# A new opening for a state-space scan with a feed-forward block: load order, halved first weights, top words on GpSimd

## The chip, the cores and the metric

The kernel runs on one core of a Trainium2 chip. The metric is the device time of one execution in microseconds (us). A core has five engines that each work through a queue of their own in order: PE (TensorE, the matrix array, with its weight loads shown as PEld), DVE (VectorE), ACT (ScalarE), POOL (GpSimd) and SP (SyncE, which here only issues DMAs). SBUF is the working memory of 128 partitions; PSUM is the memory of eight banks into which PE writes.

## The reference

A chunked scan (`mamba2_ssd`) is followed by a feed-forward block with a hard swish. Batch is 4, heads 8, sequence 768, head dimension 32, state 16; the feed-forward block has 3072 tokens, 256 model and 2048 hidden features.

```
for c in range(nc):                                  # chunks of 32 tokens
    cum = np.cumsum(la, axis=-1)                     # la = log(clip(a, 1e-6, 1))
    L = np.exp(cum[:, :, :, None] - cum[:, :, None, :]) * causal
    CB = np.einsum('bhin,bhjn->bhij', Cc, Bc)
    y_intra = np.einsum('bhij,bhjd->bhid', CB * L, xc)
    y_inter = np.einsum('bhin,bhnd->bhid', Cc, state) * np.exp(cum)[:, :, :, None]
    y[:, :, sl] = y_intra + y_inter
    state = decay_full * state + sum_j(B_j x_j * decay_from_j)
h = y_as_tokens @ w_in
out = (h * np.clip(h + 3, 0, 6) / 6) @ w_out
```

The weights `w_in` and `w_out` arrive as 64-bit floating-point numbers. The kernel sees them as pairs of 32-bit words and makes 32-bit floats of them itself.

## The kernel before

The sequence is cut into six chunks of 128 tokens, each worked in two halves of 64. For chunk c, DVE and ACT form the decays `L` (differences of cumulated logarithms, then an exponential), PE multiplies the turned B and C into the scores `cb`, DVE multiplies `L` by `cb` (L563), and PE multiplies the result with x (`mix`) and adds what comes from the state (`from_state`). ACT copies the sums y into `yT` (`keep`, L602). The feed-forward block of chunk k follows: for k = 0 it is `mlp_in` (L610, 16 hidden slices f, each with the ramp of the hard swish on ACT, L688, and its product on DVE, L693) and then `first_out` (L707). For later chunks it is done in a form with fewer products (L652 and L766), into which the scan of the next chunk is woven. The order on every engine is written out by hand: what is emitted first is first in its engine's queue.

The opening is what comes before the first `mlp_in`. Its parts are these.

- *Loads.* SP issues a, then C of chunk 0 in eight copies (`pairs_first`, L100, one for each batch and parity of the head), then x (L118) and weight pieces (L139). ACT's queue issues weight piece 0 and B ahead of its table load.
- *Differences.* `diff_mask` (L336) writes the causal mask into a PSUM bank with a matmul, `diff_less` (L348) and `diff_pick` (L357) add the differences of the logarithms, which `in_three` has split into three bf16 parts, and `diff_exp` (L365) takes the exponential. Chunk 0 uses the banks f0 to f3, chunk 1 the banks of the tags o, y0 and y1. `mask_again` (L343) writes masks a second time while PE has nothing else to do.
- *Decoding weights.* `decode(i)` makes piece i of eight (0 to 3 of `w_in`, four slices f each, 4 to 7 of `w_out`). A piece has 1024 numbers on each partition. `weights(i, n)` takes n further steps of it. ACT copies the top 16-bit word of each number (L198), DVE masks exponent and sign (L215, L217), makes the upper significand (L201) and adds the lower one (L205), ACT makes the scale in two activations (L221, L223), DVE puts the sign in (L228) and multiplies (L236). Three raw pieces fit in memory, so the load of piece i+3 waits for piece i.
- *Turning.* PE transposes B (L422), ACT copies it to `bT` (L431). DVE transposes C in squares of 32 (L465) and separates the heads of a pair into `cT` (L472). `first_eto` makes the decays from the start of the chunk, and `fade` multiplies them onto C on GpSimd (L478).

The order of the first steps in the code before is

```
weights(0, 1)
scores(0)
multiply(0)
load_w(3)
c_ps = ps.tile([P, NC, G], FP32, name="c_ps", tag="f1")
turn_cum(c_ps)
busy(1, ps.tile([P, NB * P], FP32, name="d", tag="f0"))
weights(0, 1)
weights(1, 1)
by_token(c_ps)
mix(0)
keep(0)
```

where `busy` is a matmul of the identity by itself (L490) and `turn_cum` (L316) turns the cumulated logarithms of the later chunks.

Of the kernel before, what the change touches and what calls it, by code (L numbers as in the profile page):

```python
# [20 lines left out]
def kernel(  # L21
# [63 lines left out]
    def load_bc(c):  # L85

        sl = slice(c * P, (c + 1) * P)

        def tokens_first(src, queue=nc.sync, **where):
            t = loads.tile([P, NB * NH, N], FP32, **where)
            queue.dma_start(out=t, in_=src[:, :, sl, :].rearrange("b h s n -> s (b h) n"))
            return t

        def pairs_first(src):
            t = loads.tile([P, 2, NB, 4, N], FP32, name="pairs", tag="bc")
            for b in range(NB):
                for h in range(2):
                    nc.sync.dma_start(  # L100
                        out=t[:, h, b].rearrange("s a n -> s (a n)"),
                        in_=src[b, h:NH:2, sl, :].rearrange("h (s a) n -> h s (a n)", a=4))
            return t

        if 0 < c < TURN:
            bcs[c] = [tokens_first(C, name="C", tag="bc")]
        Bs[c] = tokens_first(B, nc.scalar if c == 0 else nc.sync, name="B")
        if c == 0:
            bcs[c] = [pairs_first(C), Bs[c]]
        elif c < TURN:  # L110
            bcs[c].append(Bs[c])
        else:
            bcs[c] = [pairs_first(C), pairs_first(B)]
# [11 lines left out]
    NRAW = 3  # L125
    raws = {}

    def load_w(i, queue=nc.sync):

        raw = loads.tile([P, NK * FP * 2 * P], U32, name="raw", bufs=NRAW)  # L130
        if i < NP:
            cols = slice(2 * i * FP * P, 2 * (i + 1) * FP * P)
            src = moe_w_in[:, cols].rearrange("(k p) f -> p k f", p=P)
            dst = raw.rearrange("p (k f) -> p k f", k=NK)
        else:
            r0 = (i - NP) * FP * P
            src = moe_w_out[r0:r0 + FP * P, :].rearrange("(k p) m -> p k m", p=P)
            dst = raw.rearrange("p (k m) -> p k m", k=FP)
        queue.dma_start(out=dst, in_=src)  # L139
        raws[i] = raw  # L140

    load_w(0, nc.scalar)
    load_bc(0)
    load_x(0)
    load_w(1)
    nc.scalar.preload_act_table_set("natural_log_exp_and_others")


    ident = const.tile([P, P], FP32, name="ident")
# [37 lines left out]
    def decode(i):  # L187

        n = NK * FP * P
        top = raws[i].bitcast(U16).rearrange("p (n w) -> p n w", w=4)[:, :, 3]
        lo, hi = (raws[i].rearrange("p (n w) -> p n w", w=2)[:, :, w] for w in range(2))
        s = att.tile([P, n], U16, name="ws")
        e = att.tile([P, n], U16, name="we")
        m = att.tile([P, n], U32, name="wm")
        nc.scalar.copy(out=s, in_=top)  # L198

        def significand():  # L200
            nc.vector.tensor_scalar(  # L201
                out=m, in0=hi, scalar1=0xFFFFF, scalar2=0x100000,
                op0=ALU.bitwise_and, op1=ALU.bitwise_or)
            yield
            nc.vector.scalar_tensor_tensor(  # L205
                out=m.bitcast(FP32), in0=lo, scalar=2.0 ** -32, in1=m, op0=ALU.mult,
                op1=ALU.add)
            yield

        parts_m = significand()  # L210
        if i == 0:
            next(parts_m)
            next(parts_m)
        yield
        nc.vector.tensor_scalar(  # L215
            out=e, in0=s, scalar1=0x7FF0, scalar2=None, op0=ALU.bitwise_and)
        nc.vector.tensor_scalar(  # L217
            out=s, in0=s, scalar1=0x8000, scalar2=None, op0=ALU.bitwise_and)
        next(parts_m, None)
        yield  # L220
        nc.scalar.activation(e.bitcast(BF16), e, AF.Relu, bias=bias_hi, scale=-8.0)  # L221
        yield
        nc.scalar.activation(e, e.bitcast(BF16), AF.Relu, bias=bias_lo, scale=-1.0)  # L223
        next(parts_m, None)
        if i and i + NRAW < 2 * NP:
            load_w(i + NRAW)
        yield
        nc.vector.tensor_tensor(out=e, in0=e, in1=s, op=ALU.bitwise_or)  # L228
        m, e = m.bitcast(FP32), e.bitcast(BF16)
        if i < NP:  # L230
            dst = w_in[:, :, i * FP * P:(i + 1) * FP * P]
            m, e = (t.rearrange("p (k f) -> p k f", k=NK) for t in (m, e))
        else:
            dst = w_out[:, (i - NP) * FP:(i - NP + 1) * FP, :]
            m, e = (t.rearrange("p (k f) -> p k f", k=FP) for t in (m, e))
        nc.vector.scalar_tensor_tensor(  # L236
            out=dst, in0=m, scalar=2.0 ** -20, in1=e, op0=ALU.mult, op1=ALU.mult)

    pick = const.tile([P, G], BF16, name="pick")
    less = const.tile([P, G], BF16, name="less")
# [29 lines left out]
    def in_three():  # L273
        first = cum[:, :2 * P]
        part = split.rearrange("g c p -> g (c p)")
        nc.vector.tensor_copy(part[:G], first)
        nc.vector.tensor_tensor(out=low, in0=first, in1=part[:G], op=ALU.subtract)
        nc.vector.tensor_copy(mid, low)
        nc.vector.tensor_copy(part[G:2 * G], mid)
        nc.vector.tensor_tensor(out=part[2 * G:pad], in0=low, in1=mid, op=ALU.subtract)  # L280

    cum_d = dram.tile([NC, 2, G, HT], FP32, name="cum_d")
# [44 lines left out]

    def diff_mask(c, b):

        if c == 0:  # L330
            d = ps.tile([P, NH, HT], FP32, name="d", tag=f"f{b}")
        elif b < 2:
            d = ps_o.tile([P, NH, HT], FP32, name="d", tag="o")
        else:
            d = ps_y.tile([P, NH, HT], FP32, name="d", tag=f"y{b % 2}")
        nc.tensor.matmul(  # L336
            out=d, lhsT=ident_h, rhs=hide.unsqueeze(1).to_broadcast([P, NH, HT]),
            start=True, stop=True)
        ds[c, b] = d

    def mask_again(c, b):

        nc.tensor.matmul(  # L343
            out=ds[c, b], lhsT=ident_h, rhs=hide.unsqueeze(1).to_broadcast([P, NH, HT]),
            start=True, stop=True)

    def diff_less(c, b):
        nc.tensor.matmul(  # L348
# [153 lines left out]
                    rhs=csT[pair, b, HALF[a]], start=(a == 0 and b == 0), stop=True,  # L502
                    tile_position=(32 * q, d0), skip_group_check=True)

    def scores(c):

# [1 line left out]

        bT, cT, _ = bTs[c]
        cbs[c] = [ps.tile([P, NB, 2, HT], FP32, name="cb", tag=f"f{q}") for q in range(NQ)]
        both = [ps_y.tile([P, 2, NB, HT], FP32, name=f"y{u}", tag=f"y{u}") for u in range(2)]
        ys[c] = {(0, u): both[u][:, 0] for u in range(2)}
        sps[c] = [both[a if c else 1 - a][:, 1] for a in range(2)]
        if c:
            from_state(c, 0)
        for b in range(NB):
            for a, rows in enumerate(HALF):
                for q in range(NQ):  # L520
# [2 lines left out]
                        out=cbs[c][q][rows, b], lhsT=bT[pair, b, rows],  # L523
                        rhs=cT[pair, b, :, rows], start=(b == 0), stop=True,
                        tile_position=(32 * q, a * HT), skip_group_check=True)
        into_state(c, 0, 1)

    def into_state(c, *halves):
        xt, bs = xts[c], bss[c]
# [44 lines left out]
            op=ALU.mult)  # L574
        new_state(states[c], adds[c], later)

    def mix(c):


        xt = xts[c]  # L580
# [2 lines left out]
        for u in range(2):  # L583
# [7 lines left out]
                            tile_position=(a * HT, d0), skip_group_check=True)  # L591
            if c == 0:
                from_state(c, 1, (2 * u, 2 * u + 1))
        if c:
            from_state(c, 1)

    def keep(c):

        yTs[c] = att.tile([P, NK, NB, P], FP32, name="yT")
        for a, u in ((0, 0), (0, 1), (1, 0), (1, 1)) if c else ((0, 0), (1, 0), (0, 1), (1, 1)):  # L600
            y, dst = ys[c][a, u], yTs[c][:, u, :, HALF[a]]
            nc.scalar.copy(out=dst, in_=y)  # L602

# [243 lines left out]
            for b in bs:  # L847
                part(c, b)

    for c in range(2):  # L850
        for b in range(NB):
            diff_mask(c, b)
    for sl in ends_at:
        log_a(sl)
    row_signs()
    add_up(ends_at[0])
    in_three()
    for b in range(2):
        mask_again(0, b)
    diff(0, 0, 1)  # L860
    diff(0, 2, 3)
    weights(0, 1)
    for b in range(NB):
        diff_exp(0, b)
    first_eto()
    diff(1, 2, 3)
    weights(0, 1)
    for b in range(NB):
        ends(0, b)
    turn_b(0)  # L870
    diff(1, 0, 1)
    weights(0, 1)
    diff_exp(1, 2)
    diff_exp(1, 3)
    turn_squares(bcs[0][0], turned(0)[2])
    part_heads(0)
    fade(0, HALF[1], nc.gpsimd)
    add_up(ends_at[1])
    store_rows()
    load_w(2)  # L880
    weights(0, 1)
    scores(0)
    multiply(0)
    load_w(3)
    c_ps = ps.tile([P, NC, G], FP32, name="c_ps", tag="f1")
    turn_cum(c_ps)
    busy(1, ps.tile([P, NB * P], FP32, name="d", tag="f0"))
    weights(0, 1)
    weights(1, 1)
    by_token(c_ps)  # L890
    mix(0)
    keep(0)
    weights(1, 3)
    renew(0)
    weights(1, 1)
    load_eto(1)
    load(1)


    weave = {}  # L900
# [4 lines left out]
    for k in range(NC):  # L905
        gTs[k] = ffn.tile([P, NF, TB], FP32, name="gT")
        c, ahead = k + 1, k + 2
        if k == 0:
            for f in range(NF):
                mlp_in(k, f)  # L910
                for i in weave.get(f, []):
                    weights(i, 1)
                if f in (6, 8):
                    diff_exp(c, f // 2 - 3)
            load(ahead)
            weights(NP + 1, 1)
# [118 lines left out]
```

## Time and profile before

| what | value |
|---|---|
| median of 3 runs | 360.48 us (359.67 to 360.65) |
| profiled execution | 359.64 us, span 357.9 us |
| busy: PE, PEld | 347.9 us (97%), 300.0 us (84%) |
| busy: DVE, ACT, POOL | 221.9, 177.5, 137.9 us |
| instructions | 9350 |
| granted PE clock, mean | 0.995 |
| first `mlp_in` matmul, last one's end | 23.3 us, 51.0 us |

The profile is of one execution; its span is a little shorter than the time, which also has what lies around the span. Times on the profile's axis count from the start of the span. A line number L is one of the kernel before unless the text says otherwise. A row of the timeline has start, duration, engine, line, operation, output and inputs with their shapes, and in brackets how long the engine sat idle before it and what ended that. "PEclk" or "clock" is the clock that PE was granted, 1.00 being full.

### The profile page before, as it was taken

To read this page: it belongs to the slowest core of one execution; us is meant where nothing else is said; L and a number is where in the kernel's file an instruction comes from. 1 tells how busy PE (TensorE), PEld (TensorE's weight loads), DVE (VectorE), ACT (ScalarE), POOL (GpSimd) and SP (SyncE) were. 2 spreads that over 40 slices of the span, in tenths; PEclk is the share of its full clock that TensorE was granted. 3 is DMA by queue.
4 is the path that set the end of the run, shared out by engine and by line. 5 is a ranking of instruction groups with operands and counts; after the bars stand their busy time and mean duration, and the time that the engine had idled before them with its cause. 6 is when DMAs were issued, how large, how long until landed. Compare 5 with 4: busy or idle time off the path is not lost.

```text
span 357.9 us, 9350 instructions
## 1 busy us (share of the span) xinstructions
PE 347.9 (97%) x3936; PEld 300.0 (84%) x3936; DVE 221.9 (62%) x426; ACT 177.5 (50%) x390; POOL 137.9 (39%) x139
## 2 busy tenths in 40 slices
PE   5799999999999999999999999999999999999996
PEld 2554458888888999888999888999888999888996
DVE  6599999975887463686444687434587431588111
ACT  4678887267763730674650575560576010476100
POOL 3300000362599521099522089610068600058700
PEclk9899999999999999999999999999999999999999
DMA  8979969502924061550043560001000000000000
GB/s 166 201 277 185 266 165 127 116 4 84 155 57 60 5 136 58 81 80 2 4 113 82 74 88 2 4 2 35 26 2 1 4 3 31 29 3 0 2 29 31
DMA packets 75482, 24.97 MB, mean 70 GB/s; under 512 B 66032, under 2 KB 71824, under 8 KB 74928
## 3 DMA queue, kind: packets, MB, share of 16 engines
q1 hardware_dynamic: 71056, 23.06, 33.9%
q10 hardware_dynamic: 4384, 1.31, 1.7%
q8 instruction: 31, 0.51, 0.6%
q14 instruction: 11, 0.09, 0.1%
HBM read 21.07 MB, written 3.29 MB: 68 GB/s over the span
## 4 chain that ended last, share of the span: by engine, by line
PE 91%; DVE 3%; DMA 3%; ACT 1%; SPq 1%; issue 0%; DVEq 0%; ACTq 0%
PE ob L766 18%; PE even L652 18%; PE oa L766 18%; PE odd L652 13%; PE o L707 8%; PE h L610 8%; PE y L588 3%; PE y L500 2%; PE cb L522 2%; DMA raw<-in_moe_w_in_dram 2%; DMA pairs<-in_C_dram 1%; PE y L534 1%; SPq L100 1%; DVE odd L681 0%; DVE up L668 0%
## 5 line engine op out<-in xcount | busy, mean ns | idle before, releaser
L752 POOL TENSOR_TENSOR s<-gT 128x512 f32<-128x512 f32 x20 | 26.4, 1318 | 89.7 <-DVE gT L693 89.7
L652 PE MATMUL even<-ts,w_sum 128*128 128x256 f32 x160 | 48.2, 383 | 0.0
L667 ACT COPY even<-odd 128x512 f32<-128x512 f32 x40 | 23.0, 576 | 48.6 <-PE odd L652 46.3
L688 ACT ACTIVATE gT<-odd,half 128x512 f32<-128x512 f32 x40 | 27.5, 688 | 34.9 <-DVE odd L681 34.9
L652 PE MATMUL odd<-yT,w_in 128*128 128x256 f32 x160 | 41.1, 379 | 0.0
L766 PE MATMUL oa<-w_out,gT 128*128 128x128 f32 x320 | 38.9, 277 | 0.0
L766 PEld LDWEIGHTS oa<-w_out,gT 128*128 128x128 f32 x320 | 38.1, 192 | 0.9
L766 PE MATMUL ob<-w_out,s 128*128 128x128 f32 x320 | 37.4, 275 | 0.0
L766 PEld LDWEIGHTS ob<-w_out,s 128*128 128x128 f32 x320 | 36.5, 192 | 0.0
L652 PEld LDWEIGHTS even<-ts,w_sum 128*128 128x128 f32 x160 | 29.9, 190 | 5.3 <-ACT up L674 1.5
L693 DVE SCALAR_TENSOR_TENSOR gT<-gT,odd 128x512 f32<-128x512 f32 x40 | 27.5, 688 | 9.9 <-ACT gT L688 9.9
L652 PEld LDWEIGHTS odd<-yT,w_in 128*128 128x128 f32 x160 | 30.1, 190 | 3.9
L385 ACT ACTIVATE L<-L,cum_n 128x64 f32<-128x64 f32 x128 | 31.1, 339 | 0.0
L766 PE MATMUL ob<-t,gT 128*128 128x128 f32 x240 | 30.3, 279 | 0.0
L688 ACT ACTIVATE gT<-even,half 128x512 f32<-128x512 f32 x40 | 27.8, 695 | 4.4 <-PE even L652 4.4
L693 DVE SCALAR_TENSOR_TENSOR gT<-gT,even 128x512 f32<-128x512 f32 x40 | 27.2, 680 | 4.4 <-ACT gT L688 4.4
L766 PEld LDWEIGHTS ob<-t,gT 128*128 128x128 f32 x240 | 27.9, 192 | 1.2 <-issue 0.5
L707 PE MATMUL o<-w_out,gT 128*128 128x256 f32 x128 | 28.7, 381 | 0.0
L668 DVE COPY up<-odd 128x256 f32<-128x256 f32 x40 | 17.0, 424 | 18.6 <-ACT even L667 17.9
L610 PE MATMUL h<-yT,w_in 128*128 128x512 f32 x64 | 27.7, 594 | 0.0
L707 PEld LDWEIGHTS o<-w_out,gT 128*128 128x128 f32 x128 | 24.1, 190 | 3.7 <-issue 0.5
L563 DVE TENSOR_TENSOR L<-L,cb 128x512 f32<-128x512 f32 x24 | 15.3, 681 | 18.0 <-PE cb L522 15.5
(130 smaller groups left out, 609.8 us busy)
## 6 DMA issues: line engine op xcount, KB each, us to landing
raw<-in_moe_w_out_dram SPq DMA_DIRECT2D x4, 1024.0 KB
L<-cum_d SPq DMA_DIRECT2D x8, 512.0 KB
xt<-in_x_dram SPq DMA_DIRECT2D x6, 512.0 KB
raw<-in_moe_w_in_dram SPq DMA_DIRECT2D x3, 1024.0 KB
out_dram<-res SPq DMA_DIRECT2D x20, 128.0 KB
eto<-cum_e SPq DMA_DIRECT2D x20, 64.0 KB
B<-in_B_dram SPq DMA_DIRECT2D x5, 256.0 KB
raw<-in_moe_w_in_dram ACTq DMA_DIRECT2D x1, 1024.0 KB
```

What stands on the lines that cost most here:

```text
L385: nc.scalar.activation(Ls[c][:, b, h], Ls[c][:, b, h], AF.Exp, bias=cum_n[:, c, g:g + 1])
L563: nc.vector.tensor_tensor(out=Ls[c][:, :, hs], in0=Ls[c][:, :, hs], in1=cbs[c][q], op=ALU.mult)
L588: nc.tensor.matmul(out=ys[c][a, u][d0:d0 + D, b], lhsT=xt[rows, b * NH + h], rhs=Ls[c][rows, b, h], start=(b == 0 and a >= min(c, 1)), sto ...
L610: nc.tensor.matmul(out=h.rearrange("p r i -> p (r i)"), lhsT=w_in[:, j, f * P:(f + 1) * P], rhs=yTs[k][:, j].rearrange("p b i -> p (b i)") ...
L652: nc.tensor.matmul(out=bank[:, r], lhsT=lhsT, rhs=rhs, start=start, stop=True, skip_group_check=True)
L667: nc.scalar.copy(out=even, in_=odd[:, 1:2].to_broadcast([P, 2, 2 * P]))
L668: nc.vector.tensor_copy(out=up[:, 1], in_=odd[:, 0])
L688: nc.scalar.activation(gTs[k][:, f], h.rearrange("p r i -> p (r i)"), AF.Relu, bias=half, scale=1.0 / 6.0)
L693: nc.vector.scalar_tensor_tensor(out=g, in0=g, scalar=1.0, in1=h.rearrange("p r i -> p (r i)"), op0=ALU.min, op1=ALU.mult)
L707: nc.tensor.matmul(out=o[:, b % 2], lhsT=gTs[0][:, f, b * P:(b + 1) * P], rhs=w_out[:, f], start=(f == 0 and b % 2 == 0), stop=True, skip_ ...
L752: nc.gpsimd.tensor_tensor(out=o, in0=p_, in1=q_, op=op)
L766: nc.tensor.matmul(out=bank[:, slot], lhsT=lhs[:, j], rhs=rhs[:, j], start=(clear and j == 0), stop=True, skip_group_check=True)
```

## The change

All of it lies in the opening and in `decode`, apart from the shape of C's and B's copies in `pairs_first`, which later chunks use too.

- C's copies take one head each (all batches, 32 partitions) instead of one batch and parity (128 partitions). For chunk 0 three of the eight go on ACT's queue, behind the table load, which is now first there.
- SP's order is a, C, B, x, the two halves of weight piece 0, piece 1, piece 2. B and piece 0 leave ACT's queue.
- Piece 0 is decoded in two halves of 512. All its operations but the copy of the top words are emitted behind the multiplication of L by cb, in `weights(0, 8)` and later ones.
- GpSimd copies the top words of pieces 0 and 1 (`nc.gpsimd.tensor_copy`), behind `fade`.
- One copy of `in_three` (L279) goes from DVE to ACT.
- The differences of chunk 0 use the banks o, y0 and y1, as those of chunk 1 do; the masks of chunk 1 follow chunk 0's exponentials. Most of chunk 1's differences are emitted between the scores and the state product, whose banks (`own_banks`) they use. `busy` is gone; masks are written more often.
- `mix` is split for `turn_cum`, and `keep` into two halves between decoding steps. `load_eto` and `load` of chunk 1 move behind the slice f = 2 of `mlp_in`.

```
+        def pairs_first(src, queue=nc.sync):
             t = loads.tile([P, 2, NB, 4, N], FP32, name="pairs", tag="bc")
-            for b in range(NB):
+            for q in range(NQ):
                 for h in range(2):
-                    nc.sync.dma_start(
-                        out=t[:, h, b].rearrange("s a n -> s (a n)"),
-                        in_=src[b, h:NH:2, sl, :].rearrange("h (s a) n -> h s (a n)", a=4))
+                    (queue if h == 0 and q < 3 else nc.sync).dma_start(
+                        out=t[32 * q:32 * q + 32, h].rearrange("s b a n -> s b (a n)"),
+                        in_=src[:, 2 * q + h, sl, :].rearrange("b (s a) n -> s b (a n)", a=4))
...
-    load_w(0, nc.scalar)
+    nc.scalar.preload_act_table_set("natural_log_exp_and_others")
     load_bc(0)
     load_x(0)
+    load_first(0)
+    load_first(1)
     load_w(1)
+    load_w(2)
...
+            def words():
+                if i < 2:
+                    nc.gpsimd.tensor_copy(out=s, in_=top)
+                else:
+                    nc.scalar.copy(out=s, in_=top)
...
+        if i == 0:
+            first, second = operations(0, 2), operations(1, 2)
+            words, masks, upper, lower, above, below, sign, product = zip(first, second)
+            order = [words, (upper[0],), (masks[0],), (above[0],), (below[0],), (lower[0],),
+                     (upper[1],), (masks[1],), (sign[0], product[0]), (above[1],), (below[1],),
+                     (lower[1],), (sign[1], product[1]), (more,)]
+        else:
+            words, masks, upper, lower, above, below, sign, product = operations(0, 1)
+            if i == 1:
+                order = [(words,), (upper,), (masks,), (above, lower), (below,),
+                         (sign, product), (more,)]
+            elif i == 2:
+                order = [(upper,), (words,), (masks,), (above,), (below, lower, more),
+                         (sign, product)]
...
-        nc.vector.tensor_copy(part[G:2 * G], mid)
+        nc.scalar.copy(out=part[G:2 * G], in_=mid)
...
+    def mask_again(c, b):
+        for h in range(NH):
+            for a, rows in enumerate(HALF):
+                nc.tensor.matmul(
+                    out=ds[c, b][rows, h], lhsT=ident_h[:, rows], rhs=hide,
+                    start=(h == 0), stop=True, tile_position=(0, a * HT),
+                    skip_group_check=True)
...
+    def halves_of_next():
+        for b in range(2, NB):
+            diff_less(1, b)
+        for b in range(NB):
+            diff_pick(1, b)
+        for b in (2, 3):
+            diff_exp(1, b)
...
+    mask_again(0, 0)
+    for b in (1, 2, 3, 1):
+        diff_mask_over(0, b)
     diff(0, 0, 1)
     diff(0, 2, 3)
+    turn_squares(bcs[0][0], turned(0)[2])
+    part_heads(0)
+    add_up(ends_at[1])
+    store_rows()
     for b in range(NB):
         diff_exp(0, b)
+        ends(0, b)
+    for b in range(NB):
+        diff_mask(1, b)
+    turn_b(0)
     first_eto()
+    for b in range(2):
+        diff_less(1, b)
+    fade(0, HALF[1], nc.gpsimd)
     weights(0, 1)
+    scores(0, halves_of_next)
+    multiply(0)
+    weights(0, 8)
+    weights(1, 1)
+    c_ps = ps.tile([P, NC, G], FP32, name="c_ps", tag="f2")
+    mix(0, lambda: turn_cum(c_ps))
     weights(0, 1)
+    keep(0, 0)
+    weights(0, 3)
+    keep(0, 1)
     weights(0, 1)
+    weights(1, 2)
     by_token(c_ps)
     renew(0)
...
             for f in range(NF):
                 mlp_in(k, f)
+                if f == 0:
+                    weights(1, 2)
+                    weights(2, 1)
+                    weights(1, 1)
                 for i in weave.get(f, []):
                     weights(i, 1)
+                if f == 2:
+                    weights(1, 1)
+                    load_eto(c)
+                    load(c)
```

## The prediction

> **What bounds the kernel now.** I read the strip of forty slices on the page first, then the chain of waits, then the timelines of PE and DVE for the first 60 us.
>
> ```profile
> span 357.9 us, 9350 instructions
> PE   5799999999999999999999999999999999999996
> DVE  6599999975887463686444687434587431588111
> ```
>
> After about 23 us PE has no gap, so the end is the start of the first feed-forward product plus PE's own work. Before that the chain runs over a load:
>
> ```profile
> 8.56 4.29 DMA pairs<-in_C_dram
> ...
> 13.03 1.10 DVE csT L465
> ...
> 15.19 2.12 PE cb L522 x64
> 17.30 0.01 issue
> 17.31 1.30 DVE L L563 x2
> ...
> 23.36 16.93 PE h L610 x39
> ```
>
> The opening waits for C until 12.85, transposes it, multiplies it with B (cb), and DVE multiplies the decays L by cb from 17.31. But DVE hardly rests either in the stage that follows. Its timeline has the last step (L236) of three weight pieces here, and PE's timeline the whole stage:
>
> ```profile
> 26.77 1.23 DVE L236 SCALAR_TENSOR_TENSOR w_in<-wm,we 128x1024 f32<-128x1024 f32 x1
> ...
> 34.37 1.23 DVE L236 SCALAR_TENSOR_TENSOR w_in<-wm,we 128x1024 f32<-128x1024 f32 x1
> ...
> 41.87 1.23 DVE L236 SCALAR_TENSOR_TENSOR w_in<-wm,we 128x1024 f32<-128x1024 f32 x1
> ```
> ```profile
> 23.29 27.73 PE L610 MATMUL h<-yT,w_in 128*128 128x512 f32 x64
> ```
>
> One h record takes 27.73/64 = 0.433 us, and four hidden slices f are 16 records, 6.94 us. PE needs piece 1 (f=4) at 23.36+6.94 = 30.3, piece 2 at 37.2, piece 3 at 44.2, and w_out's first piece at 50.9. DVE delivers at 28.0, 35.6, 43.1 and 50.1. The slack is 2.3, 1.6, 1.1 and 0.8 us: **DVE is less than a microsecond from deciding this stage**.
>
> **What the Trainium skill says.** "TensorE: Matmul & The Clock Gate", Part 1: without activity over a window the array falls to half clock. The trace agrees: no matmul between 12.76 and 15.19, then half clock under cb:
>
> ```profile
> 14.00:15.00 1.00, 0.00 (x0) 0.00 (x0) 0.96 (x4) 1.00 (x2) 0.00 (x0) 1.00 0.97 110
> 15.00:16.00 1.00, 0.81 (x32) 0.84 (x40) 1.00 (x2) 0.39 (x1) 0.82 (x1) 0.53 0.95 281
> 16.00:17.00 1.00, 1.00 (x48) 0.80 (x32) 0.16 (x1) 0.00 (x0) 0.69 (x1) 0.50 0.98 401
> ```
>
> (Columns: stretch, length, busy PE, PEld, DVE, ACT, POOL, clock, DMA share, GB/s.) The next chunk's cb, at full clock, takes 1.2 us (72.95 to 74.2) against 2.0 here.
>
> "DMA: Bandwidth & Descriptors", section on the semaphore's 16: a copy uses the largest number of engines, up to 16, that divides the slowest dimension on both sides. Old C copies have 128 and 4 there, so 4 engines; new ones 32 and 32, so 16. The trace fits: from 8 to 11 us DMA is 0.37 to 0.39 busy at 43 to 83 GB/s while C is awaited.
>
> "SBUF — State Buffer", "Who interferes with whom": DVE operations with two SBUF inputs, or in a two-port mode, and GpSimd operations exclude each other for a whole instruction. The trace agrees:
>
> ```profile
> 68.23 0.94 POOL L403 TENSOR_TENSOR tmp<-state,eto 128x256 f32<-128x256 f32 x1 [51.54 <-DMA eto<-cum_e]
> ```
> ```profile
> 68.73 0.99 DVE L634 TENSOR_TENSOR w_sum<-w_sum,w_in 128x512 f32<-128x512 f32 x1
> ```
>
> The DVE row is 0.69 when alone (66.07), tmp 0.62 (86.47).
>
> **The change, part by part.** Times are on the profile's axis.
>
> 1. *Loads.* C goes first: three pieces on ACT's queue after the table load (1.28), five on SP behind a. Issues are some 0.65 each (SP's row: 602 to 718 ns), so the last leaves at about 4.6. With 16 engines I take 7 for the landing; a bound of 9.5 still hides (transposition 1.1 and halves 0.9 before 12). B: its 4096 small pieces moved at 166+108 KB between 6 and 8 before, about 2 us; issued at 5, it lands near 8.5, needed at 10.8; its issue waits for the first C copy of ACT's queue (a reused semaphore), with x and all weights behind it on SP. x moved in 3.6 us before 15; now until about 12, needed at 16.3. The w_in pieces behind it, at 400 KB per us (18 to 24 us before), land near 13.4, 14.7 and 17.4.
>
> 2. *Up to the multiplication by cb.* One DVE copy of 0.22 (L279) moves to ACT beside DVE, so the split is ready at 7.15, not 7.38. Four exponentials (2.25, from 8.22) end at 10.5. The first chunk's differences now use the banks of the second, so its last mask waits for the last exponential. Then transposes of B 0.63, bT copy 0.59, eto 0.39 (cb reuses its bank): cb starts at 12.5. PE has no gap of 2 us (the 16 small and 4 full masks fill the wait for the split), so I price cb at full clock: DVE starts L at **13.75, 3.55 earlier**.
>
> 3. *PE.* Differences of chunk 1 (0.54+1.24 from the L348/L357 rows) go into the wait behind cb, to 15.45. The state product now waits for their exponentials, since they free its banks (16.3), and all of PE's queue stands behind it; it runs 0.9; adds and mid 0.9; mix and state terms 0.9+0.6 twice, c_ps 0.4. The matmul on ident (1.12 for two records) is gone. h can start at 20.6 instead of 23.36: 2.75 earlier, **if DVE keeps up**.
>
> 4. *DVE's line.* From L to the end of piece 1 it took 28.00−17.31 = 10.7 us, of which 0.54 was waiting (L228): 10.15 of work. Three operations of piece 0, done at 7.4 to 10.1 before (0.60+1.13+0.79 start to start), now come behind L: +2.5. Halving adds five instructions; a full row less its per-element part leaves some 0.12 each: +0.6. The first gT (0.60) and upper of piece 2 (0.60) now stand ahead of piece 1's product: +1.2. ACT has adds and mid until 18.1, then two half activations of 0.65: sign waits until 19.4 though masks end at 18.5: +0.9. Sum 15.35, so piece 1 is ready at 13.75+15.35 = **29.1**, not 28.0.
>
> 5. *Top words by GpSimd.* Three copies leave ACT or hide behind L (a PSUM input, no conflict). Queued behind them on POOL is only tmp (68.23), far off. But the copy of piece 1 (128x1024) starts when its load lands, 17.4, and then keeps DVE out. No row shows it: an affine select of that size is 1.15, twice the picks copy (1.01 for 512) 2.0. I take 1.15; it shifts masks to 19.75 and the ACT steps and yT copies behind them, and 0.55 remains after the 0.9 of waiting absorbs the rest. Below: 0, if it falls into that wait. Above: 1.3.
>
> 6. *Sum.* Piece 1 at 29.65; PE, ready for it at 20.6+6.94 = 27.6, waits two microseconds and starts f=4 at 29.7 instead of 30.3: **−0.6**. Piece 3: 43.1 was 15.1 after piece 1; without the 1.2 moved ahead it is 13.9, hence 43.55; PE asks at 29.7+13.9 = 43.6. DVE and PE stay level to the end of the stage. Then w_out's second piece (56.5 against 57.8) has room, and PE carries −0.6 to the end.
>
> 7. *At no cost.* The reload for piece 4 now waits for lower at 26.5 (24.4 before), with chunk 1's eto, C, B and x behind it on SP: some 2 us later, first wanted at 66. The raw piece behind these, issued at 35, is wanted at 47.3. If that cover went, a piece would cost its lateness. Later C and B loads in the new shape run beside full PE.
>
> The profiled run took 359.64 (span 357.9), 0.84 under the median 360.48. I put the difference on the median: 359.9.
>
> **Rivals.** (a) *PE's path decides*: the split costs less, or ACT's waits vanish, so DVE delivers piece 1 by 28. For it: L starts 3.5 earlier and DVE overlaps neighbours by some 0.07. Against: 7.0 us of DVE work per piece against PE's 6.94. With 0.9 of ACT's wait and the 0.55 gone, piece 1 comes at 28.2, f=4 starts there instead of at 30.3, and piece 3 follows at 42.1: −2.0, 358.5.
> (b) *The port makes DVE late*: slower. The u16 copies read every fourth word; at four times the select's row (4.6 for piece 1, from 17.4) they keep masks of piece 1 from 22.8 and hold DVE off. Each microsecond counts one for one from a delay of 1.2 on (29.1 to 30.3); 2.7 gives +1.5, 362.0. Against: the picks copy, 1.01 for 512.
> (c) *The loads do not come in order* (B's small pieces held up): with L at 15.5 the same line gives 15.5+15.35 = 30.85, or 31.4 with the port, against 30.3: +0.6 to +1.1; 361.4.
>
> **Chances.** A measurement of this kernel tells about 0.3% (1.08 us) from no change. Main case −0.6: 0.60; (a) 0.26; (b) 0.08; (c) 0.06. Its upper bound for the port gives −1.15, so some of the main case is also "faster". Faster 0.33, within 0.57, slower 0.10. The range takes in (a)'s −2.0 and (c): 358.4 to 361.5.
>
> **What would show it.** Right: L by cb near 13.8 with full clock; h first near 20.6 to 21; a PE wait of 1 to 2 us before f=4 with w_in's L255 as releaser; POOL's copy of 1024 at 1.1 to 2.0. Wrong: h without a wait (then (a)); half clock under cb; masks or upper rows of DVE stretched by over a microsecond (b); B's transposes waiting for a DMA (c).

## The result, and the profile after

| | before | after |
|---|---|---|
| median (4 runs each, side by side) | 360.08 us (359.39 to 360.65) | 364.31 us (363.97 to 365.92) |
| profiled execution: time, span | 359.64 us, 357.9 us | 363.99 us, 362.3 us |

The ratio after to before is 1.0127 (95% interval 1.009 to 1.0165): the change made the kernel **slower by 4.2 us**, where 0.6 us less was forecast. Lines below are those of the changed kernel unless said otherwise; L647 is mix, L551 `from_state`, L675 h, L255 the last step of a weight piece.

The strip of forty slices of the changed kernel shows little of it. PE has a 7 in the third slice, where it had a 9, and is full from the fourth on; the slice with a lower clock is now the third and no longer the second:

```profile
span 362.3 us, 9394 instructions
...
PE   7779999999999999999999999999999999999996
...
PEclk9969999999999999999999999999999999999999
```

The chain of waits of the changed kernel, start and length of each piece, shows where the opening ends now:

```profile
17.36 0.72 PE y L647 x45
18.08 2.24 issue
20.32 0.34 PE y L647 x15
20.67 0.61 PE y L551 x16
21.28 0.36 PE c_ps L360 x4
21.64 1.11 PE y L647 x61
22.75 1.05 PE y L551 x16
23.80 3.73 PE h L675 x4
...
27.55 0.70 ACT gT L753
...
28.27 0.69 DVE gT L758
```

There is a piece of 2.24 us in the middle of mix called "issue": PE stands still and no semaphore that the profile shows holds it. PE's timeline of the changed kernel shows its place:

```profile
12.20 1.21 PE L571 MATMUL cb<-cT,bT 32*64 32x128 f32 x64 [0.41 <-ACT eto L427]
...
16.05 0.85 PE L593 MATMUL y<-xt,bs 64*32 64x64 f32 x64 [0.97 <-POOL ws L218]
17.36 0.72 PE L647 MATMUL y<-L,xt 64*32 64x64 f32 x49 [0.46 <-ACT adds L609]
20.32 0.34 PE L647 MATMUL y<-L,xt 64*32 64x64 f32 x15 [2.24 <-issue]
```

It stops after 49 of the 64 records of the first half of mix, and 15 follow. In the kernel before the same 64 ran through without a stop:

```profile
20.07 0.97 PE L588 MATMUL y<-L,xt 64*32 64x64 f32 x64
```

(The state product at 16.05 is put down to a POOL copy that ended at 15.49; ACT's exponentials of chunk 1, which free its banks, ended at 15.95.) Then the clock falls. Windows of the changed kernel (columns as in the prediction: stretch, length, PE, PEld, DVE, ACT, POOL, clock, DMA share, GB/s):

```profile
20.00:22.00 2.00, 1.68 (x68) 1.47 (x68) 1.41 (x3) 1.05 (x3) 0.00 (x0) 0.89 0.09 32
22.00:24.00 2.00, 2.00 (x70) 1.71 (x51) 1.62 (x3) 0.84 (x3) 0.00 (x0) 0.50 0.66 152
24.00:26.00 2.00, 2.00 (x3) 0.90 (x4) 1.93 (x7) 0.21 (x1) 0.00 (x0) 0.50 0.91 346
26.00:28.00 2.00, 2.00 (x3) 0.67 (x2) 0.08 (x1) 0.45 (x1) 0.00 (x0) 0.50 0.13 47
28.00:30.00 2.00, 2.00 (x6) 0.89 (x5) 1.74 (x2) 1.97 (x3) 0.00 (x0) 0.90 0.00 0
```

From 21.6 to 28.4 PE runs at half speed. A record of h takes 0.93 us there (3.73 for four in the chain above), and took 0.43 before. DVE's timeline of the changed kernel shows the lateness handed on, for gT of the first slice stands ahead of the last steps of piece 1; the three pieces that were at 26.77, 34.37 and 41.87 now start at

```profile
28.27 0.69 DVE L758 SCALAR_TENSOR_TENSOR gT<-gT,h 128x512 f32<-128x512 f32 x1 [2.18 <-ACT gT L753]
...
31.33 1.23 DVE L255 SCALAR_TENSOR_TENSOR w_in<-wm,we 128x1024 f32<-128x1024 f32 x1
...
38.34 1.23 DVE L255 SCALAR_TENSOR_TENSOR w_in<-wm,we 128x1024 f32<-128x1024 f32 x1
...
45.83 1.23 DVE L255 SCALAR_TENSOR_TENSOR w_in<-wm,we 128x1024 f32<-128x1024 f32 x1
```

The whole difference, from start to start. Mix begins at 17.36. At full clock and without the stop its first half, the state terms and c_ps take 1.00+0.61+0.36 (the timeline at 17.36 to 18.08 and 20.32 to 21.57), and its second half and the state terms behind it take 0.79+0.61 (from run e6 below, 20.19 to 21.59). So h would begin at 20.7, which is an estimate from these rows. It begins at 23.73: 2.24 of stop and 0.76 of half clock. From there to `first_out` (54.22) it is 30.49 instead of 27.57 (23.29 to 50.86 before), 2.92 more. Of that some 2.5 is half clock, by an estimate (the 4.67 us up to 28.4 hold 5.0 records of 0.93 us, which take 2.2 us at full clock), and 0.22 is a wait for piece 3. Against before: 20.73−23.29 = −2.56, +2.24, +0.76, +2.92 makes the +3.36 that `first_out` shows. By 76.2 the difference is 0.29 larger, in chunk 1's scan. A second "issue" stop, at 287, adds 0.48. With some 0.2 unplaced, PE's last group starts 4.29 later (357.01 against 352.72).

### The profile page after: what moved, and what is told of

Same layout as the page of the kernel before. It is cut to its first block, busy times and chain, and to the rows that moved or that the text cites. A ratio compares the mean times of both kernels' runs of the same rounds, so it can differ in the third digit from the quotient of the medians.

```text
span 362.3 us, 9394 instructions
## 1 busy us (share of the span) xinstructions
PE 351.4 (97%) x3952; PEld 300.7 (83%) x3952; DVE 223.8 (62%) x431; ACT 175.8 (49%) x391; POOL 140.9 (39%) x142
## 4 chain that ended last, share of the span: by engine, by line
PE 77%; DVE 13%; ACT 3%; DMA 3%; issue 2%; SPq 1%; POOL 0%; DVEq 0%; ACTq 0%
PE ob L831 18%; PE even L717 18%; PE oa L831 17%; PE odd L717 13%; PE y L647 3%; DVE gT L758 2%; DVE wm L234 2%; DMA raw<-in_moe_w_in_dram 2%; PE y L551 2%; PE o L772 2%; PE cb L571 1%; DVE w_out L255 1%; PE y L593 1%; ACT we L239 1%; DVE we L245 1%
## 5 line engine op out<-in xcount | busy, mean ns | idle before, releaser
L831 PE MATMUL ob<-t,gT 128*128 128x128 f32 x240 | 30.5, 280 | 0.5 <-issue 0.5
L675 PE MATMUL h<-yT,w_in 128*128 128x512 f32 x64 | 30.3, 635 | 0.2 <-DVE w_in L255 0.2
```

Of the source, the lines that this page charges most:

```text
L675: nc.tensor.matmul(out=h.rearrange("p r i -> p (r i)"), lhsT=w_in[:, j, f * P:(f + 1) * P], rhs=yTs[k][:, j].rearrange("p b i -> p (b i)") ...
L831: nc.tensor.matmul(out=bank[:, slot], lhsT=lhs[:, j], rhs=rhs[:, j], start=(clear and j == 0), stop=True, skip_group_check=True)
```

## The experiments

**What was suspected.** The page has 31 packets of one DMA queue called "instruction" (columns: packets, MB, share):

```profile
q8 instruction: 31, 0.51, 0.6%
```

0.51 MB in 31 packets are 16 KB each; PE's 3952 matmuls and 3952 weight loads are 7904 instructions, 255 for each packet. The theory: PE's own instructions come over the DMA engines in blocks of 16 KB, 256 instructions, and PE had used up one block before the next was there. In the quarter of a microsecond from 17.75 to 18.0, the DMA view of the changed kernel has one of these packets beside the weight traffic:

```profile
DMA packets 19, 0.09 MB, mean 360 GB/s; under 512 B 0, under 2 KB 0, under 8 KB 18
...
q1 hardware_dynamic: 18, 0.07, 73.2%
q8 instruction: 1, 0.02, 26.0%
```

PE goes on at 20.32. In the kernel before, the packet was at 18.0 to 18.25 and PE came to its boundary (the 62nd record of mix, as e4 and e7 show) at about 21.0, so nothing stopped. The second stop of the changed kernel has its packet too, at 284.75 to 285.0; PE goes on at 287.13. Rivals: the stop belongs to mix (its tiles, its operands), or the loss lies in DVE's order, or in GpSimd's port. For each run the table has the stretch in which the packet appeared (0.25 us, its start), the restart of PE, the stop, the start of h, and the time. All but the last column is of one profiled execution. The ratios given at the runs are to the kernel before, measured side by side.

| kernel | packet | PE goes on | stop | h | median, us |
|---|---|---|---|---|---|
| before | 18.0 | no stop | 0 | 23.29 | 360.08 |
| after | 17.75 | 20.32 | 2.24 | 23.73 | 364.31 |
| e1 hold piece 2 | 17.25 | 19.57 | 2.00 | 23.74 | 363.69 |
| e2 15 matmuls fewer | 19.25 | 21.78 | 3.96 | 25.35 | 365.44 |
| e3 gT later | 19.5 | 22.05 | 4.10 | 26.20 | 365.29 |
| e4 before + C shape | 19.5 | 21.95 | 2.52 | 25.50 | 363.28 |
| e5 hold pieces 1, 2 | 16.75 | 19.54 | 1.62 | 22.82 | 363.20 |
| e6 before + C shape + hold | 17.0 | 19.36 | 0.26 | 21.59 | 358.66 |
| e7 before, load moved | 20.75 | 23.25 | 3.00 | 25.94 | 364.13 |
| e8 before + hold | 18.25 | 20.77 | 0.41 | 23.00 | 359.45 |

In all of them that have a stop, PE goes on 2.3 to 2.8 us after the packet is seen. What differs is when the packet comes.

**e1: the load of piece 2 held back.** A small DMA that needs `mid` stands on SP ahead of the load.

```
-    load_w(2)
...
+    nc.sync.dma_start(out=hold, in_=mids[0][:, 0, 0:8])
+    load_w(2)
```

> The changed kernel with one difference: the load of weight piece 2 leaves SP only after ACT has made mid (about 17.9 us), so no weight traffic runs between some 17.5 and 19 us. Theory 1 (PE stops at 18.08 because its next block of instructions, the 16 KB packet of the instruction queue seen at 17.75, waits behind weight traffic): the stop of 2.24 us shrinks below 1 us, the clock stays full, h starts near 21.5, and the time falls by 2.5 to 4 us against the changed kernel, to within 1 us of the kernel before. Theory 2 (the block comes late whatever else moves, because PE asks for it too late in a run of short matmuls): the stop stays at 2 us or more and the time stays within 0.7 us of the changed kernel. Theory 3 (a hidden wait on another engine's work): the same as theory 2, with the stop at the same matmul.

Ratio to before 1.011 (1.0087 to 1.0133). The stop went from 2.24 to 2.00 only, and under 1 was forecast: piece 1 was still on its way until about 17.5. A miss as a cure.

**e2: fifteen matmuls fewer ahead of mix.** The differences start from one full mask instead of sixteen small ones.

```
-    mask_again(0, 0)
-    for b in (1, 2, 3, 1):
+    for b in (0, 1, 2, 3, 1):
         diff_mask_over(0, b)
```

> The changed kernel with the sixteen small masks of chunk 0 replaced by one full one, so that PE has 15 matmuls and 15 weight loads fewer ahead of mix. Theories 1 and 2 (PE runs out of fetched instructions at a place that its instruction count sets): the stop moves 15 matmul records later, from the 49th to about the 64th record of the first half of mix or into the state terms behind it, its length between 1.5 and 2.3 us, and the time within 1 us of the changed kernel. Theory 3 (a hidden wait on another engine): the stop stays at the 49th record of mix.

PE's timeline of this kernel:

```profile
16.96 0.86 PE L647 MATMUL y<-L,xt 64*32 64x64 f32 x64 [0.46 <-ACT adds L609]
21.78 0.92 PE L551 MATMUL y<-csT,mid 32*64 32x64 f32 x16 [3.96 <-issue]
```

The stop moved from the 49th record to the 64th, by the fifteen taken away: it is tied to PE's count of instructions, not to what they do. It also became longer than the 1.5 to 2.3 forecast, since the packet came later. Ratio 1.0158 (1.0137 to 1.0179).

**e3: piece 1's last steps ahead of gT.**

```
-                mlp_in(k, f)
                 if f == 0:
                     weights(1, 2)
                     weights(2, 1)
                     weights(1, 1)
+                mlp_in(k, f)
```

> The changed kernel with the ramp and product of the first hidden slice (gT, f = 0) queued behind piece 1 of the weights on ACT and DVE. If DVE's line is held up by the first gT waiting for PE (2.18 us of idle time at 26.1): piece 1 is ready 2 to 3 us earlier (about 30 instead of 32.56), and the time falls by 0.5 to 1.5 us, the rest staying with PE, which starts h at 23.7 at half clock. If the loss is PE's alone, the time stays within 0.4 us of the changed kernel though piece 1 comes earlier. If DVE's line carries all of it, the time falls by 2 us or more.

Ratio 1.0149 (1.0117 to 1.0181). The stop was 4.10 this time, at the same 49th record, although nothing ahead of it differs. So the packet's time varies from one execution to the next, by 1.75 us here, and a small difference between two stops of single traces shows nothing. The time of this run says nothing of DVE's order either. Piece 1 ended 5.75 us after h began (31.95 against 26.20), where in the changed kernel it was 8.83 (32.56 against 23.73).

**e4: the kernel before with the new shape of C's copies alone.**

```
-            for b in range(NB):
+            for q in range(NQ):
...
-                        out=t[:, h, b].rearrange("s a n -> s (a n)"),
-                        in_=src[b, h:NH:2, sl, :].rearrange("h (s a) n -> h s (a n)", a=4))
+                        out=t[32 * q:32 * q + 32, h].rearrange("s b a n -> s b (a n)"),
+                        in_=src[:, 2 * q + h, sl, :].rearrange("b (s a) n -> s b (a n)", a=4))
```

> The kernel before with C's eight copies in the new shape (one head each, 32 partitions) and nothing else of the change. If C's lateness before came from copies on few DMA engines: C lands 2 to 4 us earlier than 12.85, the transposition starts by 10.5, the multiplication by cb by 15.5, and the time falls by 1 to 2.2 us. If C was late because it stood behind weight piece 0 and B: it lands within 1 us of before and the time moves by less than 0.7 us.

Ratio 1.0101 (1.0076 to 1.0126). C came 1.15 us sooner, and not the 2 to 4 forecast (transposed at 11.88, not 13.03; L by cb at 15.54, not 17.31), and PE ran into the stop, at the 62nd record of mix. One part of the change, which makes the opening earlier, is enough to lose 3.7 us (363.28 against 359.54 beside it).

**e5: pieces 1 and 2 of the changed kernel held until chunk 1's exponentials.**

```
-    load_w(1)
-    load_w(2)
...
+    nc.sync.dma_start(out=hold, in_=Ls[1][:, 3, 0, 0:8])
+    load_w(1)
+    load_w(2)
```

> The changed kernel with weight pieces 1 and 2 held back on SP until ACT has made the exponentials of chunk 1 (about 16 us), so that DMA runs dry at about 14.5. Runs so far: the stop always ends 2.3 to 2.5 us after the instruction packet starts, and the packet started at 17.25 to 19.5, each time near the end of a stretch of weight traffic. Theory 1 (the packet that PE asks for at some 14 us waits until the weight traffic in front of it is through): the packet starts by 15.2, the stop in mix is under 0.3 us, the clock stays full through mix, h starts at 20.8 to 21.5, and the time falls by 3 to 5 us against the changed kernel, to 0 to 1.5 us under the kernel before. Theory 2 (the packet comes late whatever the traffic): packet at 17 or later, a stop of 2 us or more, time within 1 us of the changed kernel.

Ratio 1.0095 (1.0069 to 1.012). Little moved from 14.5 to 17.0 (a DMA share of 0.02 to 0.35), the packet came at 16.75, and still the stop was 1.62, where under 0.3 was forecast, and half clock followed. Less traffic was not a full cure.

**e6: e4 with pieces 2 and 3 held until `mid`.**

```
     multiply(0)
+    hold = dram.tile([P, 8], FP32, name="hold")
+    nc.sync.dma_start(out=hold, in_=mids[0][:, 0, 0:8])
+    load_w(2)
     load_w(3)
```

(The line `load_w(2)` ahead of `scores(0)` goes.)

> The kernel before with C's new shape, and with weight pieces 2 and 3 held back until ACT has made mid (about 17.5 us). Theory 1: the packet starts at about 16.5 instead of 19.5, when piece 1 is through; PE meets no stop at the 62nd record of mix, h starts near 21 to 21.5, and the time is 1.2 to 2.4 us under the kernel before. Theory 2: packet at 19 or later, a stop of 2 us or more, and a time 3 to 4 us over the kernel before, as with the new shape alone.

PE's timeline of this kernel:

```profile
15.26 0.30 PE L534 MATMUL y<-xt,bs 64*32 64x64 f32 x4
15.90 0.82 PE L534 MATMUL y<-xt,bs 64*32 64x64 f32 x60 [0.34 <-issue]
16.73 0.43 PE L316 MATMUL c_ps<-ident,pre 32*128 32x32 f32 x4
17.09 1.12 PE L490 MATMUL d<-ident 128*128 128x512 f32 x2
18.14 0.95 PE L588 MATMUL y<-L,xt 64*32 64x64 f32 x62
19.36 0.30 PE L588 MATMUL y<-L,xt 64*32 64x64 f32 x2 [0.26 <-issue]
...
20.19 0.86 PE L588 MATMUL y<-L,xt 64*32 64x64 f32 x64
20.98 0.68 PE L500 MATMUL y<-csT,mid 32*64 32x64 f32 x16
21.59 27.73 PE L610 MATMUL h<-yT,w_in 128*128 128x512 f32 x64
```

Two short stops, and between them 60+4+2+62 = 128 matmuls, a block. (The packet ahead of the first of them was seen at 12.75, some 3 us before, under heavy traffic.) The clock stays full and h begins at 21.59. 358.66 against 359.74 beside it, ratio 0.9963 (0.9937 to 0.9989): **0.4% faster than the kernel before**, and 5.6 us under the median of the changed one. The 1.1 us gained are just under the 1.2 forecast. C's shape has a gain, once PE's instructions are not behind weights.

**e7: the kernel before with one load moved.** `load_w(2)` follows `load_w(1)`; nothing else.

> The kernel before with one line moved: weight piece 2 is issued right behind piece 1, so that the gap in the traffic at 18.0 us, in which the instruction packet started, is closed until about 20.5. Theory 1: the packet starts at 20 or later, PE stops at the 62nd record of mix (reached at about 21) for 1.3 us or more, and the time rises by 1.5 to 4 us. Theory 2: packet near 18, no stop, time within 0.4 us of the kernel before.

```profile
23.25 0.30 PE L589 MATMUL y<-L,xt 64*32 64x64 f32 x2 [3.00 <-issue]
```

Ratio 1.0079 (1.0032 to 1.0125). More weight traffic alone, at the time when the block is wanted, makes the loss in a kernel that has no other part of the change. Neither e4 nor e7 has the new order on DVE or copies on GpSimd, so the loss needs neither. The kernel before may itself be near it: two of its seventeen executions beside e5 to e7 took 363.49 and 363.72, as long as runs with a stop, with a granted clock of 0.98; no trace of them is there to say whether PE stopped.

**e8: the hold of e6 in the kernel before, C's old shape.**

> The kernel before with pieces 2 and 3 of the weights held back until mid exists, and C's old shape kept. It fills the fourth corner of a square with the kernel before, the new shape alone and the new shape with the hold. Fetch theory (PE's instructions come in 16 KB blocks that wait behind weight traffic): before already had its block in time, so the hold has nothing to cure: block at 18.0 or a little earlier, no stop of PE, h at 23.3 to 23.5, time within 0.3% of before (359.0 to 361.0). Rival (the hold helps by itself, because a calmer memory speeds C, B or DVE): 1 us or more faster, as the new shape with the hold was.

Ratio 0.9998 (0.9981 to 1.0015). The forecast of no change held, that of no stop was off by 0.41. Shape alone +1.0%, hold alone nothing, both −0.4%: the hold takes away what the shape brought on.

**e9: 60 more matmuls ahead of the differences, in e5.**

```
     for b in (1, 2, 3, 1):
-        diff_mask_over(0, b)
+        mask_again(0, b)
```

> The changed kernel with pieces 1 and 2 held until chunk 1's exponentials, and with the four full masks ahead of the differences written as sixteen small matmuls each: 60 instructions more on PE, in a stretch where it waits for the split. Fetch theory: the boundary moves 60 records ahead, from the 49th of mix to about the 53rd of the state product; asked for at about 14.7, while little moves, the block is there at 15.0 and PE goes on near 17.3, a stop of at most 0.9 us beside waits that PE has anyway; full clock; mix near 18, h at 21 to 21.8. Then the rest of the prediction applies: piece 1 of the weights decides f=4, at about 29 to 30, and the time is 357.8 to 360.0. Rival (a stop belongs to mix itself, such as its tiles or its operands): the stop stays in mix, 1.6 us or more, half clock, 363.

```profile
15.95 0.77 PE L591 MATMUL y<-xt,bs 64*32 64x64 f32 x54 [0.97 <-POOL ws L216]
17.62 0.35 PE L591 MATMUL y<-xt,bs 64*32 64x64 f32 x10 [0.91 <-issue]
...
24.56 0.68 PE L645 MATMUL y<-L,xt 64*32 64x64 f32 x31 [2.66 <-issue]
```

The boundary went where it was expected (after the 54th record of the state product, the 53rd forecast; stop 0.91). Not foreseen was the next one: 10+64+16+4+33 = 127 records on, in mix again, with the held weights now in its way (packet at 22.0, stop 2.66). Full clock was forecast, and half clock came at 17.8, ahead of mix. 369.47 us, ratio 1.0276 (1.023 to 1.0322). The forecast of time failed; the count of 128 held again, but for one record.

**e10: e9 with e3's order of gT.**

> The kernel with the shifted boundary, and the remaining steps of weight piece 1 emitted ahead of the first slice's product gT. Theory (once PE comes late, gT f0 ahead of piece 1 on DVE hands PE's lateness to the weights): piece 1 is ready 0.6 to 1.5 us earlier than with the shift alone, PE's wait before f=4 shrinks by as much, time 0.3 to 1.0 us lower. Rival (piece 1 is set by its load and its top words, so the order on DVE is of no account): piece 1 within 0.3 us of the shift alone, and the same time.

367.56 us, ratio 1.023 (1.0183 to 1.0277). The first stop, again after the 54th record, was 2.57, with nothing changed ahead of it against e9's 0.91. Its packet came at 16.5, a microsecond after the traffic had ended (a DMA share of 0.14 from 15.5 to 16.5), so weight traffic is not all that makes a packet late. Piece 1 ended 4.8 us after h began (31.41 against 26.64), in e9 8.8 (35.04 against 26.21). But PE waits for a weight piece in neither, and the first `first_out` comes after 30.5 us of h in both: at half clock PE itself is slower than DVE. The two profiled spans are 368.2 and 368.3, while the medians, of four runs each, are 1.9 apart (0.3 to 1.0 forecast); with stops that vary this much the traces don't say why. What the order of gT costs in a run without a stop stays open.

**e11: the cost by itself.** 1424 small matmuls behind the last product of the kernel before, six loads of 1 MB behind the 33rd group of sixteen. This is one execution.

```
+    tail(32, "f0")
+    d = tail(1, "f1")
+    seen = const.tile([P, 8], FP32, name="seen")
+    nc.vector.tensor_copy(seen, d[:, 0, 0:8])
+    hold = dram.tile([P, 8], FP32, name="hold")
+    nc.sync.dma_start(out=hold, in_=seen)
+    for i in range(6):
+        load_w(i)
+    tail(56, "f2")
```

> The kernel before with 1424 small mask matmuls added on PE behind its last product: first 528 while hardly anything moves, then 896 beside six weight loads of 1 MB, which wait for the 33rd group of sixteen. Their results are used by nothing. It measures the disputed cost by itself. Fetch theory: PE stops once in each 128 matmuls (128 matmuls and 128 weight loads are 256 instructions of 64 bytes, a block of 16 KB), with no semaphore named; asked for half a block ahead, the block takes about 2.4 us without traffic, of which 64 matmuls of 0.02 us cover 1.3, so the quiet stops are about 1 us; beside the loads they are 2 to 4 us. Rival 1 (instructions are fetched far ahead whenever the memory is quiet): no stop in the first 528, some in the rest. Rival 2 (the stops belong to mix and the state product, not to the number of instructions): no stop at a fixed distance in either part.

PE's timeline of the middle of that tail; SP issues the loads from 371.16 to 382.84:

```profile
362.59 2.21 PE L1016 MATMUL d<-hide,ident_h 128*64 128x64 bf16 x128 [0.89 <-issue]
366.32 2.22 PE L1016 MATMUL d<-hide,ident_h 128*64 128x64 bf16 x128 [1.51 <-issue]
369.77 2.21 PE L1016 MATMUL d<-hide,ident_h 128*64 128x64 bf16 x128 [1.24 <-issue]
373.50 2.21 PE L1016 MATMUL d<-hide,ident_h 128*64 128x64 bf16 x128 [1.51 <-issue]
379.43 2.21 PE L1016 MATMUL d<-hide,ident_h 128*64 128x64 bf16 x128 [3.71 <-issue]
385.35 3.62 PE L1016 MATMUL d<-hide,ident_h 128*64 128x64 bf16 x128 [3.71 <-issue]
```

One stop after each 128 matmuls, no semaphore, 0.9 to 1.8 us while nothing else moves (the last two of the tail, 1.79 and 1.51, are not shown), 3.7 us beside the loads, and 2.57 where the loads end. The packets were seen at 360.0, 363.5, 367.25, 371.0, 377.0 and 382.75, which is 2.4 to 2.8 before each restart. Both rivals fall. 128 matmuls of this size last 2.2 us; a block costs 3.5 to 3.7 us in quiet, 5.9 beside weight loads. At half clock, where 128 of them last 3.6 us, two blocks in a row (256 matmuls from 391.54) went through without a stop between them.

## Why the prediction was wrong

**Step 2 held, and step 1 in the main.** L by cb began at 13.46 (13.75 forecast), cb took 1.21 at full clock (1.2), and C, which the transposition at 6.42 did not wait for, was earlier still than the 7 taken. The two halves of piece 0 and piece 1 landed some 1.4 later than forecast (POOL's copies start at 14.85, 16.19 and 18.74 as they land; 13.4, 14.7 and 17.4 forecast). DVE did not wait for them, but it means weight traffic at the very time when PE's instructions were wanted.

**Step 3 is the step that failed**: "h can start at 20.6". Its engine work was well sized, since without the stop h would begin at 20.7 by the sum above, but it priced PE's path as engine work and semaphores only. The time for PE's instructions to come stood at nothing, without a reason; it was 2.24 us of stop, and the half clock that followed. (The terms as listed add up to 21.5, not 20.6, because rows overlap by some tenths.) The change took away what had covered the fetch of PE's instructions. Before, mix came late enough, behind a matmul on ident of 1.12 us and a wait for L. With the 2.3 to 2.8 us of the other runs, the block of 18.0 was there between 20.3 and 21.0, and PE came at 21.0: less than a microsecond of room, by this estimate. After, PE came to the boundary at 18.08, with a packet at 17.75. That room was the hidden limit of the opening, and no row of the profile before shows it: a stop that doesn't happen has no line. "If DVE keeps up" was the wrong condition.

**Step 7 gave no cost to the weights' new order**, and looked for what is late behind the loads. It did not ask what else uses the DMA engines: the 1 MB loads now move at 400 to 430 GB/s through 15 to 19, when the block is wanted. e7 shows that cost without the rest of the change, e6 against e4 shows it taken away. e5 shows that quiet alone does not do, with 1.62 left. How much of the 2.24 is traffic is not shown: e5's stop is 0.6 shorter, but e3's is 1.9 longer with nothing changed ahead of it. A reading that fits e11 is that PE asks for the next block when half of one is left: 64 of its matmuls last 1.1 us, and in quiet its packets came within 0.4 us of that place, beside loads 2.5 us after it. No experiment took this apart, and e10's first packet, late in quiet, does not fit it. No run of the changed kernel was free of the stop, so that it is the cause there rests on the counts, the packets and the sum above, and on e4, e6 and e7, which are the kernel before with one or two parts changed.

**Step 3 also counted on full clock to the end.** The Trainium skill, "TensorE: Matmul & The Clock Gate", Part 1, gives about 3.4 us without activity as the window for half clock. The prediction's own trace had half clock after a gap of 2.42, and the changed kernel was to have no gap of 2 us. Here half clock followed stops of 1.62 (e5), 2.24 and 2.52 us (e4), and in e9 one of 0.91 that came soon after a wait of 0.97; the measurement decides. It lasted 6.8 us in the first three (21.6 to 28.4 after, 21.7 to 28.6 in e4), 10.2 in e1 and e3, and 13.7 in e9 and e10, which have a second stop. After stops of 0.26 and 0.41 the clock stayed full. In the changed kernel it cost 0.76 ahead of h and some 2.5 behind it, more than the stop itself.

**Step 4** gave 29.1 for piece 1; it was ready at 32.56. DVE's own work was well priced: 14.6 us from L on (19.1, less three waits of 0.60, 0.90 and 2.18 and the 0.8 of step 5), against 14.45. The wait of 0.60 is the one forecast as 0.9. The 2.18 that DVE waited for gT are PE's lateness and the half clock, not DVE's work. Most of the 0.90 is PE's lateness too, handed on by ACT, whose second scale step stands behind the copies of y:

```profile
20.74 0.37 ACT L667 COPY yT<-y 128x256 f32<-128x256 f32 x1 [0.93 <-PE y L647]
...
21.59 0.72 ACT L242 ACTIVATE we<-we,bias_lo 128x512 uint16<-128x512 bf16 x1
```

In e3, with a stop of 4.10, the same wait of DVE was 2.87. Without the 2.18 and the 0.90 piece 1 would be ready at about 29.5 by subtraction, against 29.65 with step 5. The "1.2 ahead" was priced as DVE work of 0.6 and 0.6, and not as an entry by which PE's lateness gets into DVE's line. At half clock that line decided little, though: PE waited 0.22 in all.

**Step 5**: the copy of 128x1024 took 1.10 (1.15 forecast), those of 512 took 0.64 and 0.82. The sharing of the port shows on DVE:

```profile
16.52 0.64 DVE L225 TENSOR_SCALAR ws<-ws 128x512 uint16<-128x512 uint16 x1
...
18.33 0.29 DVE L225 TENSOR_SCALAR ws<-ws 128x512 uint16<-128x512 uint16 x1
19.23 0.89 DVE L245 TENSOR_TENSOR we<-we,ws 128x512 uint16<-128x512 uint16 x1 [0.60 <-ACT we L242]
...
22.35 0.43 DVE L245 TENSOR_TENSOR we<-we,ws 128x512 uint16<-128x512 uint16 x1 [0.90 <-ACT we L242]
```

The same operation took 0.64 beside POOL's copy and 0.29 without, 0.89 and 0.43 (POOL's copies ran from 16.19 to 17.01 and from 18.74 to 19.84): 0.8 us in all, against the 0.55 that the prediction kept of it. No run took this apart.

**Step 6 and the rivals.** Without the stop, piece 1 at 29.5 against the 30.3 at which PE begins f=4 before would have left the forecast of −0.6 about right; that is arithmetic, and no run shows it. None of the rivals was the case: PE's path (a) did decide, but in the other direction; the port (b) cost 0.8, far from the 2.7 that (b) took; the loads (c) came in order. The rival that was missing had its sign in the page before: the queue of instructions in part 3.

## What to carry to other kernels

Where an opening is a row of many small matmuls, count them: in these runs each 128 with their weight loads were a 16 KB block that had to come over the DMA engines, and a shorter path brought PE to the boundary sooner while the block came hardly sooner. Before making such a stretch denser or moving loads forward into it, look for the packets of the instruction queue in narrow windows, and compare them with the time at which PE gets to that place; hold a large load back by a small DMA where they meet, and measure, since it helped in e6 and did not cure e1 and e5. An idle of PE that is put down to "issue" with no engine named, 128 matmuls after the last such idle, is a sign of this wait. The word alone is not enough: in e1 and e2 the wait of 0.98 ahead of the state product, the one that ACT's exponentials end in the changed kernel, is put down to "issue" too.

## What was not expected of the hardware

- PE's instructions come in blocks of 256 over the DMA engines. From the packet to the restart it took 2.3 to 2.8 us in the runs of the table, and dense small matmuls went at 128 in 3.5 to 3.7 us even when nothing else moved (e11).
- Weight loads delay such a block: stops of 0.9 to 1.8 us in quiet were 3.7 us beside loads (e11). A block can come late in quiet too (e10).
- Adding instructions, or taking them away, in one place moves a stop to another (49th to 64th record in e2; e9). With such an edit to masks alone the median went from 363.2 (e5) to 369.47 (e9).
- Half clock came with stops of 1.6 us and more in the opening, and in e9 with one of 0.91 soon after a wait of 0.97; it lasted 6.8 to 13.7 us. In the tail of e11, stops of 1.5 and 1.8 us between dense matmuls left it full, and of two stops of 3.7 us the first left it full and half clock began in the second (at 384.3). What exactly the clock counts stays open.
